# A new task order and new engine choices for the attention half of a fused attention and two-layer expert kernel

## The chip, the cores and the metric

The kernel runs on one core of one Trainium2 chip. The metric is the device time of one execution in microseconds (us). The kernel before took 1091.92, 1090.54 and 1091.52 us in three runs; their median is 1091.52 us.

## The reference

```python
def _attn_ref(q, k, v, tau):                     # 4 batches, 8 heads, 576 rows, head size 64
    scores = (1.0 / np.sqrt(64)) * np.matmul(q, k.transpose(0, 1, 3, 2))
    thresh = np.max(scores, axis=-1, keepdims=True) - tau
    scores = np.where(scores >= thresh, scores, -1e9)
    attn = np.exp(scores - np.max(scores, axis=-1, keepdims=True))
    attn = attn / (np.sum(attn, axis=-1, keepdims=True) + 1e-09)
    return np.matmul(attn, v)

def _moe_ref(x, w_gate, w_val, w_out):           # x: 2304 x 512, d_ff 1536
    gate = 1.0 / (1.0 + np.exp(-(x @ w_gate)))
    return (gate * (x @ w_val)) @ w_out

def _moe2_ref(x, w_in, w_out):                   # d_ff 2048
    h = x @ w_in
    return (h * np.cos(h)) @ w_out
```

The attention output is brought to 2304 x 512 and goes through the two layers in turn. Everything is float32, and the weights come as 64-bit floats.

## The kernel before

To keep float32 precision at the matmul's faster rate, an operand is split into a rounded high part and the rest, the low part, and a product is summed from high x high, high x low and low x high. Each split costs an activation (high part, ScalarE) and a subtraction (low part, VectorE or GpSimd).

The program has two halves. The first does attention for all 16 pairs of heads, and beside it the first products of layer one for the batches that are done. The second does the rest of layer one and all of layer two. Each half is a list of tasks of one engine each. `put_out` records the tasks engine by engine; where a string of letters is given for an engine (`ORDER`), the tasks are put out in just that order: a letter is a kind of task, and its n-th mention is the n-th task of that kind. The planner's own costs then have no say. An engine works off its queue in order, so a task that waits holds up all that stand behind it. The second half is ordered by another table (`LATER`).

In the first half a pair of heads has nine queries of 128 rows (144 in all). For one of them:

- S (TensorE, line 959): scores, 4 matmuls of 288 columns (6 for every ninth query) into one of two score banks `s`.
- M (VectorE, 965): the row's extreme `sm`. E (ScalarE, 970): exp from the bank into `p`. Y (any engine: 813, 815 or 817): the threshold. K (VectorE, 973): masks `p` by comparing the bank with the threshold. After K the bank is free for the next query but one.
- T, t (TensorE, 989 and 996): turns `p` by matmuls against the identity into one of two banks `t`. H, h (ScalarE, 899): the high part of the turned rows into `PT` or `LT`. The low part is made in one of three ways, by a letter in `LOWS` (for T) or `LOWS_L` (for t): V, a subtraction on VectorE (task L or l, line 910); G, a copy on ScalarE (task C, 914) and a subtraction on GpSimd (task G, 919); T, a matmul by minus the identity onto the bank (task N or n, 903) and a second activation (task O or o, 906).
- V (TensorE, 1056): the product with the values, four to a pair. Where `SHARED` has an S it takes 14 matmuls that write the result once (task a, 1017); else 9 that leave it in two halves, to be added by F (ScalarE, 1026) and A (VectorE, 1031).
- At the end of a pair the sums are inverted and spread, U scales `x` (1147), X and x split it into `xs_a` (1163 or 1165, and 1169). Then P (TensorE, 564 to 566) can run: products of layer one, three matmuls of 512 columns each, 144 of them; e (ScalarE, 1214) takes a sum out to `st` and it goes to memory.
- Before a pair, its q, k and v are split: s, Q, q for the queries (688 or 690, `qsplit` at 703 or 705, `ql` at 710), J and j for the keys (`khi`, `klo`), Z and z for the values (`vn`). Which engine does each is a letter for every pair in `WHERE`; that of Y is in `YS`.
- D (TensorE, 825): four matmuls on the identity that fill time, as many after a query's S as `FILL` says. b (ScalarE, 1183): loads the table for the sigmoid.

SyncE issues the transfers (loads, copies of split parts into place, `LZ`, sums) in an order of its own.

Of the kernel before, what the change touches and what calls it, by code (L numbers as in the profile page):

```python
# [52 lines left out]

ORDER = dict(
    PE=(
        "SDDDDSTSNDDDSTSNtTSnTStNSTTNSTtDDNSTStVNTtSSTBVtTSNSTTSVTtSSTVtNNSTStVnTTtNSTVBStSTVSTVTNSNtSTTNNSPtTPPStPST"
        "VTVStNSPTPPBSPPTPSStPTVTPStSVTTPSPtPTSPtPTPTVtSSTVPBTPtSPSTPPTPStSTVTVtSSTVNtVTTSPSPTPtSPPTBPSStPTPPSTtPSVTT"
        "SVtSPTPtSTVTVtSSPTBPPTtPSSTTVPtSPSTTVSPtSPPTPStTPTPVtTSSBVTPStPSPTPTSSPVtPSTPTPtVSPtTSPVTTSVtSPTPBPtSSTPPTTS"
        "StVPTTSStVVtTVnSTTSPtTPPBSPSPTPtSTVTtSVSTPTPPSTtPPSPTStVPTtPSSBTPVTtSPSTVTPSStPTPTSPSVPStPTPtSTPTVtPTPSSBPtT"
        "VPSSTTVtTVSTPSPTtPSPtVSTTVStPTSBPtPTPPSTPSVtTVSTTSPNNtPPSTSPPTPtSStPTPVTPSSBVTPtSSPTPTPStPTVSPTtSPVStPTPVTPT"  # L60
        "StSPTPBVtPTSSVTTVSPTtSPTPtSPPTPtSSPTTVSPtSTVPTBPStPTSPtTSVTVTSSVPtPTPtPPTPTPVtPBVBV"
    ),
    ACT=(
        "JQJQEYQsHEEOwHEOhECHo6EHhOEwHHHEOHhEOh6pHhEwEOHhCa6HEREhHwOEH6CHEEaahHwEYYHEHhOO6hHFhpEYoHHEhOwECFHRZhEYaHE6"
        "FwEHYaHOOhEHHH6OOwEhYhECehH6eHEEHFwFhOpEH6eREECweeHhEEHHe6hFEEYFHHHpwhheEHCEhe6CHHeFwhEHC6RFEHheHEEYHeheCEEF"
        "HHHFhhHYEOhFEFHpHECHheEERHeEehEHeYChHeEEHHCFEHhhFCHehHEpEFhHCFEHCREHheeHEEFChHEeHHEHFhhEeHCehEYHECHephFHCEER"
        "YFHhYsEEHeeCEHEFheHEHJhheHhFHEepEYFCHHEhYFEHYRehYHEEHeHChEEeCHHFhhEHFQFhHEopFHHCEhYHEReeEEHChHEeFHEhFHsHHQeY"
        "EHhhEeeHhpEEFChHesRHEEhCHeFEEYFHCHhEQEHHeYEHFEhhCHEhpHeHEFhHREEhCFHeYHHCEFhEHHFHEYhhHEYhEpeFCHHEFhHRCeEHCEeC"
        "heHEEhFHCFHHHEEOOhheCEHYEHeehEHEeFphCHXREEFHheEHEeHCheEZCHFEhheHHFEphHeECHHFhZeHEREeHhCYFEEFHHCFhECHHeHhEhEC"
        "heHpYEYEHCHehFHEEHRFhEHChHCeEECFHHHFFEhEhCHbhpeXHHXhFeFFX"  # L70
    ),
    DVE=(
        "jqMjqKqMMKKM4MK5MKYKMlMYYK4LL5MKYKllMMYlK4K5IlMMLKKM4l5KMMLKKlMML4K5KllMLMKLAYIlM4K5KMAMKLxlMA4KK5MYlMKxLM4K"
        "llK5MMYlLKKAM4lAI5KMLMYKK4M5MlKKLLMMAlKKALLLM4llM5IlKKLMA4l5MKAYKLMlMLKKLlMMKKALLAMllMKlAYKMLYAKIMLMlYKKLMMK"
        "lLKMMYlKKMALLllKAMMlLKKAMIlAMYKKlLMMLYKKMlAMKLYKAMLLlYlKMMlKYLKIlMMAKKAMLMlKKMMYKLAlMYLKKllLLMlAMLKKIMALMlAK"
        "KLMlMLKKLMlMYKKMMAllLLAKALKMLAMYlIKLKMMKYKMlYLKMLAYlMAKLLLMKllLKMMlLYKKIlAMMYLKKMjYlMAKKLMMlYKAKMLMKLLYAKllM"
        "YlMLLKIKlLAMMYYKKlMMALqKAlKMLLLAKMllMKLlMKAILKAlMMYYKKMlMYKYAKlAMLMKKMlYMlKKLMlMLKKIlAMMYKYKLMMAlKLMYlYKKMzA"
        "lKlMLLMAlYYILKKLlAMMYLYKKMMAlKYAKLMAlYKMLYLMllKKlMMKKLMMAlLIKKLMYlKAlMYMKYKALLAMMllAKKlILxlLAAUxAUxx"
    ),
    POOL=(  # L80
        "JJQYJYjYqZYzG7csQq7YJjYY7GYZ7YYzcGsQJ7qjUYsGXz7YQcUX7YqYJG7Y7jYYsYcQGZYqz7YJGY7GY7GjYUXZxYYsczQUXxGqJZYzYGjs"
        "cQGYJGYYqYGGYGjYsUcXYGQxZzJqGUXGxYjZYGQGqczYYZjsUXxYGzYcGGYYZUXxqzGYJjcGqYYGYJGcZzYqUGZzJjGYsGQGYZcUzXXxYxYJ"
        "GjGGGcYUYGsJjQGqYUYXxxGYGcsYQJqGzjGGGUcZGYGzUYGYGGGcYYGURRX"
    ),
    SP=(
        "10001W2uuuyWyuyy0ddssssW1uduuuW2ssssdyyrrW0y1RyssssRW2uu0uussssWrr1ddRRWyyy2yssssuuWgguu0Wssdssyydgg1WgyygDs"
        "sssrrWyggu2RRuugdrssrssuyd0RRyssssyggDu1u2d0gusygsrugss1dryyygsssysgRg2uuRu0dssssdg1ygurrgsgyyssRRsDuugg0ddu"
        "s2sssr1urygyyyDgg0ssssu2uRRyugyugDysssrrysgdg2ssssRRdu1gug0ssdrssdgguu2yDDgsyyrysssg10uuddRgssRssuugygyyy12s"
        "usssdguDrdryug0Ryussssr2rggD1RyssssdyRguu2uyRssss1yyudy0gsgDgssrrgRRs1gdys0gsdyrgrssguuuuDssyyDssgg2dgRRssss"
        "gg2uugrrdyyyuyusssRgsgRDssDssssssgrrRRgggDD"  # L90
    ),
)
# [1901 lines left out]
```

## Time and profile before

| | value |
|---|---|
| median of three runs | 1091.52 us |
| the profiled execution's own time | 1094.26 us |
| its span, first to last instruction | 1092.5 us |
| TensorE / VectorE / ScalarE / GpSimd busy | 98% / 83% / 70% / 50% |
| first product of layer one (line 564) begins | 70.84 us |
| first matmul of the second half (line 1441) begins | 384.95 us |

The span is that of one profiled execution; 1.8 us of the execution's time lie around it. The busy shares are means over both halves. A matmul's duration in the rows runs from its start to its modelled end, and matmuls overlap; what one costs the engine is the distance from its start to the start of the next.

### The profile page before, as it was taken

The numbers are of one execution on the slowest core, as the hardware profiler recorded it, in microseconds if no ns is written. First come the engines' busy times: TensorE is split into PE (matmuls) and PEld (weight loads), VectorE is DVE, ScalarE is ACT, GpSimd is POOL, SyncE is SP. The second block draws the span as 40 slices with busy tenths as digits, with TensorE's granted clock in tenths as the row PEclk, the third lists the DMA queues.
The fourth block names the chain that finished last, engine by engine and source line by source line (L and its number), as shares of the span: only waits on it lengthen the run. The fifth ranks groups of instructions, "written<-read, shape, count | busy, mean of one in ns | idle before, by whom it ended". The sixth has DMA issues, their size and how long they took to land.

```text
span 1092.5 us, 17726 instructions
## 1 busy us (share of the span) xinstructions
PE 1071.8 (98%) x5784; PEld 912.5 (84%) x5784; DVE 909.9 (83%) x1647; ACT 764.4 (70%) x1488; POOL 543.7 (50%) x521
## 2 busy tenths in 40 slices
...
GB/s 194 235 225 250 213 225 225 205 232 216 198 207 203 90 231 280 329 331 315 299 228 244 163 191 138 291 203 210 173 154 154 157 175 169 193 193 262 277 203 87
DMA packets 94494, 234.06 MB, mean 214 GB/s; under 512 B 13258, under 2 KB 21570, under 8 KB 84674
## 3 DMA queue, kind: packets, MB, share of 16 engines
...
q8 instruction: 46, 0.75, 0.3%
...
## 4 chain that ended last, share of the span: by engine, by line
PE 51%; DVE 2%; DMA 1%; ACT 1%; issue 0%; ACTq 0%
PE h L1441 5%; PE h L1442 5%; PE h L1443 5%; PE h L1630 4%; PE h L1631 4%; PE h L1632 4%; PE o L1750 4%; PE o L1751 4%; PE o L1752 4%; PE o L565 3%; PE o L566 3%; PE o L564 3%; DMA early<-gd 1%; PE o L1840 1%; PE o L1842 1%; PE o L1841 1%
## 5 line engine op out<-in xcount | busy, mean ns | idle before, releaser
L1676 POOL TENSOR_TENSOR g<-raws,g 128x512 fp32r<-128x512 f32 x68 | 94.7, 1402 | 139.7 <-ACT g L1675 117.6
L965 DVE TENSOR_REDUCE sm<-s 128x1 f32<-128x576 f32 x144 | 106.5, 751 | 8.9 <-PE s L959 7.2
L973 DVE SCALAR_TENSOR_TENSOR p<-s,sm,p 128x576 f32<-128x576 f32 x128 | 102.7, 812 | 9.3 <-ACT p L970 3.9
L1441 PE MATMUL h<-x,w 128*128 128x256 f32 (+1 forms) x304 | 101.4, 333 | 0.4 <-DVE raws L1718 0.4
L1442 PE MATMUL h<-x,w 128*128 128x256 f32 (+1 forms) x304 | 101.3, 333 | 0.0
L1443 PE MATMUL h<-x,w 128*128 128x256 f32 (+1 forms) x304 | 101.3, 333 | 0.0
L970 ACT ACTIVATE p<-s,sm 128x576 f32<-128x576 f32 x128 | 93.8, 742 | 9.8 <-DVE sm L965 9.0
L899 ACT ACTIVATE PT<-t 128x512 fp32r<-128x512 f32 (+1 forms) x160 | 86.1, 557 | 15.1 <-PE t L989 10.3
L959 PE MATMUL s<-kk,qh 128*128 128x288 f32 x320 | 92.4, 320 | 2.9 <-DVE p L973 2.5
L1056 PE MATMUL v<-PT,vn 128*128 128x256 f32 (+3 forms) x532 | 84.7, 302 | 0.2 <-ACT st L1214 0.2
L919 POOL TENSOR_TENSOR PT<-praw,PT 128x512 fp32r<-128x512 f32 x51 | 66.7, 1307 | 35.4 <-ACT praw L914 16.9
L1760 DVE TENSOR_TENSOR y<-o,y 128x512 f32<-128x512 f32 x120 | 78.6, 681 | 6.1 <-PE o L1752 5.9
L959 PE MATMUL s<-khi,ql 128*128 128x288 f32 x288 | 81.0, 295 | 0.6 <-DVE ql L670 0.6
L989 PE MATMUL t<-ident,p 128*128 128x128 f32 x512 | 77.0, 276 | 3.2 <-DVE PT L910 1.7
L1750 PE MATMUL o<-g,w 128*128 128x512 f32 x196 | 76.8, 392 | 0.5 <-ACT o L1766 0.5
L1751 PE MATMUL o<-g,w 128*128 128x512 f32 x196 | 76.4, 390 | 0.0
L1752 PE MATMUL o<-g,w 128*128 128x512 f32 x196 | 76.3, 389 | 0.0
L1630 PE MATMUL h<-form,w 128*128 128x512 f32 x192 | 75.0, 390 | 0.5 <-ACT side L1599 0.5
L1056 PEld LDWEIGHTS v<-PT,vn 128*128 128x128 f32 (+1 forms) x532 | 73.3, 186 | 2.2 <-DVE x L1031 0.5
L1631 PE MATMUL h<-form,w 128*128 128x512 f32 x192 | 74.7, 389 | 0.0
L1632 PE MATMUL h<-form,w 128*128 128x512 f32 x192 | 74.7, 389 | 0.0
L1675 ACT ACTIVATE g<-raws 128x512 fp32r<-128x512 f32 x106 | 64.3, 624 | 13.1 <-DVE raws L1718 8.3
...
## 6 DMA issues: line engine op xcount, KB each, us to landing
...
```

Source lines behind the costliest of these rows:

```text
L959: nc.tensor.matmul(s[:, half, 0:HALF], qq, keys[:, half * HALF:half * HALF + HALF], start=(i == 0), stop=(i == len(mms) - 1),)
L965: nc.vector.tensor_reduce(self.sm()[:, 0:1], self.s()[:, :, 0:HALF], axis=AX.XY, op=ALU.min)
L1056: nc.tensor.matmul(o, w, x, start=z == 0, stop=z == len(steps) - 1)
L1441: nc.tensor.matmul(o, w_hi, x(0, c), start=begin, stop=False, **late)
L1442: nc.tensor.matmul(o, w_hi, x(1, c), start=False, stop=False, **late)
L1443: nc.tensor.matmul(o, w_lo, x(0, c), start=False, stop=c == KC - 1, **late)
L1630: nc.tensor.matmul(ps(), of(0, c), hi, start=fresh and c == 0, stop=False, skip_group_check=True)
L1631: nc.tensor.matmul(ps(), of(0, c), lo, start=False, stop=False, skip_group_check=True)
L1632: nc.tensor.matmul(ps(), of(1, c), hi, start=False, stop=c == 1, skip_group_check=True)
L1750: nc.tensor.matmul(ps(), of(0, c), hi, start=begin, stop=False, skip_group_check=True)
L1751: nc.tensor.matmul(ps(), of(0, c), lo, start=False, stop=False, skip_group_check=True)
L1752: nc.tensor.matmul(ps(), of(1, c), hi, start=False, stop=True, skip_group_check=True)
```

## The change

The change replaces tables of letters and nothing else: the strings of `ORDER` for all five engines, `LOWS`, `LOWS_L`, `SHARED`, `WHERE`, `YS` and `FILL`. The arithmetic, the tiles, the planner and the second half's table are the same. A few lines show the kind:

```diff
 ORDER = dict(
     PE=(
-        "SDDDDSTSNDDDSTSNtTSnTStNSTTNSTtDDNSTStVNTtSSTBVtTSNSTTSVTtSSTVtNNSTStVnTTtNSTVBStSTVSTVTNSNtSTTNNSPtTPPStPST"
+        "SDDDDSTSNDDDSTtSNTSnDtTnSNSTTNSTDDDStTSNtVTSStTVBTtSNnSTTStVTSTSVtNSNStTVTTStNBTVSStTnVTSTVTtSnSTNtSPTPPSPTS"
...
 SHARED = (
-    "SSS. .S.S .... .... .... .... .... .... .... .... .... .... .... .... .... .... "
+    "SS.S S..S .... .... .... .... .... .... .... .... .... .... .... .... .... .... "
...
-    Q="APPPPPPPPPAAAPPP", q="DPPPPPPPPPPPPDPP", J="APPPPPPPPAPPPPPP", j="DPPPPPPPPPPDPPPP",
+    Q="APAPAAAAAPAAPPPP", q="DPPPPPPPPPPPPPPP", J="APPPPPPPPPPPPPPA", j="DDPPPPPPPPPPPPPP",
```

Counted over the first half, the tables change these numbers of tasks:

| engine | before and now |
|---|---|
| TensorE | N 18 to 11 (512 columns: 12 to 9; twice 256 columns: 6 to 2), n 3 to 6, D 9 to 11 |
| ScalarE | O 18 to 11, o 3 to 6, C 51 to 54, Q 6 to 11, s 4 to 5, Z 3 to 4, X 4 to 5, Y 29 to 27 |
| VectorE | low parts of 256 columns 26 to 30 and of 128 columns 61 to 58, U on full rows 0 to 2, x 6 to 7, q 4 to 3, Y 53 to 57 |
| GpSimd | G 51 to 54, Q 12 to 7, U 15 to 13, s 11 to 10, Z 13 to 12, X 12 to 11, x 10 to 9, q 14 to 15, Y 62 to 60 |

A bank's T with two halves has two pieces of each kind. The shared products stay five (three of 256 and two of 320 columns).

VectorE near the program's start, before the change; `klo` is the low part of a pair's keys, `wt` a piece of the layer's weights:

```order
L517 TENSOR_SCALAR wt<-wraw 128x512
L965 TENSOR_REDUCE sm<-s 128x1
L973 SCALAR_TENSOR_TENSOR p,sums<-s,sm,p 128x576
L520 SCALAR_TENSOR_TENSOR wt<-we,wt 128x512
L965 TENSOR_REDUCE sm<-s 128x1
```

The same place now:

```order
L965 TENSOR_REDUCE sm<-s 128x1
L973 SCALAR_TENSOR_TENSOR p,sums<-s,sm,p 128x576
L710 TENSOR_TENSOR klo<-raw_k,khi 128x640
L520 SCALAR_TENSOR_TENSOR wt<-we,wt 128x512
L965 TENSOR_REDUCE sm<-s 128x1
```

The second pair's `klo`, which GpSimd made before, now stands in VectorE's queue.

TensorE at the 86th to 88th query before, from the first instruction behind the 86th query's scores to the last of the 87th's (scores `s_3510`); behind them stand a T, a V, a T and a t, and then the 88th's scores, which take the 86th's bank:

```order
L564 MATMUL m_3477<-xs_a_98,w_554 128x512
L565 MATMUL m_3477<-xs_a_98,w_554 128x512
L566 MATMUL m_3477<-xs_a_98,w_554 128x512
L989 MATMUL t_3489<-ident_65,p_3366 128x128 x4
L996 MATMUL t_3508<-ident_65,p_3366 128x128
L959 MATMUL s_3510<-kk_2990,qh_1_100 128x288 x2
L959 MATMUL s_3510<-khi_2947,ql_1_102 128x288
```

The same place now, from the last instruction of the 86th's scores (`s_3511`) to the first of the 88th's (`s_3576`):

```order
L959 MATMUL s_3511<-khi_3020,ql_1_102 128x288
L959 MATMUL s_3523<-kk_3154,qh_1_100 128x288 x2
L959 MATMUL s_3523<-khi_3020,ql_1_102 128x288
L989 MATMUL t_3539<-ident_65,p_3479 128x128 x4
L989 MATMUL t_3546<-ident_65,p_3479 128x128 x4
L1056 MATMUL v_3556<-PT0_3270,vn_3033 128x320 x8
L1056 MATMUL v_3556<-LZ_3459,vn_3033 128x320
L959 MATMUL s_3576<-kk_3154,qh_1_100 128x288
```

Between a query's scores and the next in the same bank there stood two P tasks, two turns, a t, a V and one query's scores more; now two turns, a V and one query's scores.

ScalarE at the end of the first half, before:

```order
L1183 ACT_TABLE_LOAD
L1183 ACTIVATE one<-halfpi 128x1
L899 ACTIVATE LT<-t 128x128
L1069 ACTIVATE sums<-sums 128x9
L1214 ACTIVATE st<-m 128x512
L1163 ACTIVATE xs_a<-x_97 128x512
L899 ACTIVATE PT_5725<-t 128x4x128
```

And now:

```order
L899 ACTIVATE PT_5789<-t 128x4x128
L899 ACTIVATE LT<-t 128x128
L1163 ACTIVATE xs_a<-x_97 128x512
L1214 ACTIVATE st<-m 128x512
L1026 ACTIVATE half<-v 64x256
L1026 ACTIVATE half<-v 64x320 x2
L1183 ACT_TABLE_LOAD
L1183 ACTIVATE one<-halfpi 128x1
L1163 ACTIVATE xs_a<-x_97 128x512
```

The table load stood ahead of the last high parts; now only the last `xs_a` stands behind it in this half. TensorE ends the half with six P tasks behind the last query's scores, where it had eight.

## Rows read from the trace of the kernel before

**Rows 1.** The page: busy time, share of the span, instructions.

```profile
span 1092.5 us, 17726 instructions
...
PE 1071.8 (98%) x5784; PEld 912.5 (84%) x5784; DVE 909.9 (83%) x1647; ACT 764.4 (70%) x1488; POOL 543.7 (50%) x521
```

**Rows 2.** Stretches: length; busy PE, PEld, DVE, ACT, POOL; clock, DMA, GB/s.

```profile
8.00:71.00 63.00, 54.70 (x375) 46.56 (x374) 59.49 (x128) 56.29 (x122) 46.16 (x54) 1.00 0.82 223
...
71.00:380.00 309.00, 304.82 (x1978) 266.28 (x1977) 277.31 (x646) 264.58 (x578) 205.47 (x238) 1.00 0.75 208
```

**Rows 3.** Waits of TensorE, first 388 us: releaser, total, times, longest.

```profile
PE s L959 <- DVE p L973: 2.5, 6, 0.7
```

**Rows 4.** TensorE in order of time: start, duration, what.

```profile
8.44 1.91 PE L825 MATMUL warm<-ident 128*128 128x128 f32 x16
...
202.31 0.40 PE L566 MATMUL m<-xs_a,w 128*128 128x512 f32 x1
202.55 0.39 PE L564 MATMUL m<-xs_a,w 128*128 128x512 f32 x1
...
203.23 1.03 PE L989 MATMUL t<-ident,p 128*128 128x128 f32 x8
204.18 0.40 PE L959 MATMUL s<-kk,qh 128*128 128x288 f32 x1
```

**Rows 5.** VectorE by line and shape, first 388 us: busy, mean ns, idle before.

```profile
L965 DVE TENSOR_REDUCE sm<-s 128x1 f32<-128x576 f32 x144 | 106.5, 751 | 8.9 <-PE s L959 7.2
L973 DVE SCALAR_TENSOR_TENSOR p<-s,sm,p 128x576 f32<-128x576 f32 x128 | 102.7, 812 | 9.3 <-ACT p L970 3.9 <-POOL sm L815 2.5 <-ACT sm L813 0.3
L910 DVE TENSOR_TENSOR PT<-t,PT 128x512 fp32r<-128x512 f32 x65 | 44.5, 685 | 5.8 <-ACT PT L899 5.0
L910 DVE TENSOR_TENSOR LT<-t,LT 128x128 fp32r<-128x128 f32 x61 | 17.2, 281 | 2.7 <-ACT LT L899 2.3
...
L817 DVE TENSOR_SCALAR sm<-sm,taus 128x1 f32<-128x1 f32 x53 | 10.6, 205 | 0.4
...
L710 DVE TENSOR_TENSOR klo<-raw_k,khi 128x640 fp32r<-128x640 f32 x1 | 1.9, 1939 | 0.0
...
L710 DVE TENSOR_TENSOR vn<-raw_v,vn 128x640 fp32r<-128x640 f32 x1 | 0.8, 812 | 0.0
```

**Rows 6.** ScalarE by line and shape, same stretch and columns.

```profile
L970 ACT ACTIVATE p<-s,sm 128x576 f32<-128x576 f32 x128 | 93.8, 742 | 9.8 <-DVE sm L965 9.0
...
L703 ACT ACTIVATE qsplit<-raw_q 128x576 fp32r<-128x576 f32 x3 | 2.1, 686 | 0.0
```

**Rows 7.** In time: the first product of layer one and its releaser.

```profile
69.82 0.69 DVE L1169 TENSOR_TENSOR xs_a<-x,xs_a 128x512 fp32r<-128x512 f32 x1
...
70.84 0.40 PE L564 MATMUL m<-xs_a,w 128*128 128x512 f32 x1
```

**Rows 8.** In time: VectorE's `klo`, and what GpSimd ran beside it.

```profile
245.74 1.94 DVE L710 TENSOR_TENSOR klo<-raw_k,khi 128x640 fp32r<-128x640 f32 x1
...
245.71 1.29 POOL L919 TENSOR_TENSOR PT<-praw,PT 128x512 fp32r<-128x512 f32 x1 [2.26 <-ACT PT L899]
```

**Rows 9.** In time: the end of the first half.

```profile
370.89 0.28 PE L1056 MATMUL v<-LZ,vn 128*128 128x256 f32 x1
371.48 0.47 PE L564 MATMUL m<-xs_a,w 128*128 128x512 f32 x1 [0.31 <-DVE x L1031]
...
375.00 1.28 ACT L1183 ACT_TABLE_LOAD   x1
...
379.88 0.40 PE L566 MATMUL m<-xs_a,w 128*128 128x512 f32 x1
380.36 0.41 PE L1103 MATMUL t<-ident,bc 128*128 128x128 f32 x2
380.97 1.43 PE L1056 MATMUL v<-PT,vn 128*128 128x320 f32 x8 [0.19 <-ACT st L1214]
...
384.95 0.49 PE L1441 MATMUL h<-xs_a,w 128*128 128x512 f32 x1
```

More of the change, by code (lines that the diff above doesn't have):

```diff
@@ L55 @@
     PE=(
-        "SDDDDSTSNDDDSTSNtTSnTStNSTTNSTtDDNSTStVNTtSSTBVtTSNSTTSVTtSSTVtNNSTStVnTTtNSTVBStSTVSTVTNSNtSTTNNSPtTPPStPST"
[L57 to L60, printed above, removed]
@@ L61 @@
-        "StSPTPBVtPTSSVTTVSPTtSPTPtSPPTPtSSPTTVSPtSTVPTBPStPTSPtTSVTVTSSVPtPTPtPPTPTPVtPBVBV"
+        "SDDDDSTSNDDDSTtSNTSnDtTnSNSTTNSTDDDStTSNtVTSStTVBTtSNnSTTStVTSTSVtNSNStTVTTStNBTVSStTnVTSTVTtSnSTNtSPTPPSPTS"
+        "tVTVtSnSPTPBPSSTPPtTPSSTtPVPTSTPVtPSTtPSPTTPVPtTSSBPVTPtSSPTTPPStPSVTTVtSSTVtNVTTSPtSPPTPSBPStTPPSSPPTTPSStV"
+        "TTVPStPTStVTTVSPtSPTPBSPTtPSTTPSVTtVStPSTPPTPSSTPtVtTPSBSTPVtPTSSPTPTSStVPTPSTtVSPTPtSTPTPtVSTSPVTBPtSSPTPTS"
+        "tSVTPSPVtTSVTStVTTPStPTPBSPPtTPSSTTVStTVTPSPPStPPTPtSSPTVTPStSTPBVTPtSSPTPTSVtSPTTPSSVtPSTPSPtTPTVtSPTBPStPV"
@@ L62 @@
+        "TPSSTTVtTVTStPSPTPStPTVSTSVPtTPPSPSBTPtSVTTPStSTVPTSPtPSTtPPSTTPPStPVTSBPSPVTStPSPPTTSPVTtSPSPtTVSPTPtVSTTSP"
+        "tVPBTStSPTPVTSSTVPtTSTPPSPPtTPStPTVTSPtTSVPBTPStTPStPTVSVTSVtPTPSPTPPtPTPTPtVBVBV"
     ),
     ACT=(
-        "JQJQEYQsHEEOwHEOhECHo6EHhOEwHHHEOHhEOh6pHhEwEOHhCa6HEREhHwOEH6CHEEaahHwEYYHEHhOO6hHFhpEYoHHEhOwECFHRZhEYaHE6"
-        "FwEHYaHOOhEHHH6OOwEhYhECehH6eHEEHFwFhOpEH6eREECweeHhEEHHe6hFEEYFHHHpwhheEHCEhe6CHHeFwhEHC6RFEHheHEEYHeheCEEF"
-        "HHHFhhHYEOhFEFHpHECHheEERHeEehEHeYChHeEEHHCFEHhhFCHehHEpEFhHCFEHCREHheeHEEFChHEeHHEHFhhEeHCehEYHECHephFHCEER"
@@ L67 @@
[L67 to L70, printed above, removed]
+        "QJJQEYQsHEEwOHhEOEHCo6hEHwOoEHHHYOEQHE6hhHpEYhwEOHCa6hHEERHhwOoEHCHaEYhEF6HHwEYEHhhOpOahCHE6HHEhOEwRHaZhFH6E"
@@ new lines @@
+        "EYoFCHHwEahHo6EHOEHhhQwECH6eeHphEEHFhCowFEYERCHe6HEEhHeewCEEHFh6eHHEYQwHhhehHpCFEeHH6EFehCHwREE6HhesFEHEHehe"
+        "EYEFHCHHFQhhHEhOFEHpCFHhYEEeHReEEhCeHEEHHeQehEFHEHHFhheCHhEFHEHCpFhEeHsERECHhQeHHeEEFhCHFhhHHEEHCepeHEhEhZHF"
+        "eRHEEheHCEECFHHeEhEFYHCeHhhHFEHChEpHeEHFheHCEEYFRHhesEEHCHheXEQFHCEYEeFHHhhFHphCEFHHEheHYREEYeChHQeEHCHEFhCH"
+        "FHHEeEYhheEHehEYpHEHFehZHCEERHehFEEYHHYhEFECeHHEEHhhpCHFEYhHeHEFhRHshEEHFeHCHEFhECHZhhHHEFCHEhEpFeHEHCYFhHEC"
+        "eERHehEEHHehFEEFHHCHhhEeYhHepYEHCEeHehECFRHEEYFeHhEEeHHCYEeHFhCJEhehHHFEHYEheFHHCphEEFReChHEHEFHeEHCFhEHHHEe"
@@ L71 @@
+        "eEhhHpChEHCHFehHCEERCHFHChhEeCEHYFFCHEFEhHHHhCEhXepHHhXeFXFFbX"
     ),
     DVE=(
[L73 to L76, printed above, removed]
@@ L77 @@
-        "YlMLLKIKlLAMMYYKKlMMALqKAlKMLLLAKMllMKLlMKAILKAlMMYYKKMlMYKYAKlAMLMKKMlYMlKKLMlMLKKIlAMMYKYKLMMAlKLMYlYKKMzA"
-        "lKlMLLMAlYYILKKLlAMMYLYKKMMAlKYAKLMAlYKMLYLMllKKlMMKKLMMAlLIKKLMYlKAlMYMKYKALLAMMllAKKlILxlLAAUxAUxx"
+        "qjMjqKqMYMKK4MYMKj5MKYKM4MKLL5MKLKMllMKl4K5MMIlLKKM4Y5KMLMKlKAMMLKKll4MMl5YYKILMlKYK4L5MAMLKKMAL4Y5KMMKxLLYM"
+        "K4Y5lKlMMlLIKKAMM4AKK5MMYLKKlLM4M5KAlMLKKLLll4M5lAMKLLIKAlMM4Y5KKLlMMAYYKLKMlLMKKALLMAllYMlKAxKMALMlIKKLMMYK"
+        "KlMMYYKKLLMMlKALKLLlAlMMlYKALKMIAlKMLMYYKKlMYLLMKUAlKMAMYLLKKllMMIYLlKKlLAMYMLYKKlMMYKKAMLYMlKAKLllMLMKAlMYL"
@@ L79 @@
+        "KLKMAMlIYKKALMlMKKMlLKMAMKKALLllMAMlIxKLLAKlMLMKKlMMKLKlAMYALLKMMllKKLMMlYKLKLMlAIMYYKKLMAMlKKLMLlMKYKAMMYKL"
+        "LYKllMAMlKILLAlKLMYMlKKLAMMLYYKlAKMllLLKMAYMYKlKMAMILAlKKMYKMLMlKKLLMlAMYYKKAMLLllMKlLMIKKMYLlKMYAMKKAMYlLMK"
+        "LMKKlMAMKlLLlMAKLlKAMLMlIYKKMMYYALKKlMMALKAlKMLLLMKlYlMlKKLAIMMlYKUKAMlYlMKzKAAMMYYKKLLAMYllKlILxLlAxUAAUxx"
     ),
     POOL=(
-        "JJQYJYjYqZYzG7csQq7YJjYY7GYZ7YYzcGsQJ7qjUYsGXz7YQcUX7YqYJG7Y7jYYsYcQGZYqz7YJGY7GY7GjYUXZxYYsczQUXxGqJZYzYGjs"
-        "cQGYJGYYqYGGYGjYsUcXYGQxZzJqGUXGxYjZYGQGqczYYZjsUXxYGzYcGGYYZUXxqzGYJjcGqYYGYJGcZzYqUGZzJjGYsGQGYZcUzXXxYxYJ"
@@ L83 @@
-        "GjGGGcYUYGsJjQGqYUYXxxGYGcsYQJqGzjGGGUcZGYGzUYGYGGGcYYGURRX"
-    ),
-    SP=(
[L86 to L90, printed above, removed]
+        "JJQqYJYG7YcsZzYqJ7YZGYY7jsGQYqc7YzJjU7sGXzY7xGUYXc7JjqYYGZ7YGGsYz7YYc7GqYJGY7jY7UXZxzGYcGJUXYqjYZsYGzYJcjYGq"
@@ new lines @@
+        "YZGYzGGqYcJXYGxUYXGxjGYscGQzGYYqJZGjzGUYYYGqcYGxUYXsGYJjZGYYGqcGzJYjYUGsczQGqJUjYZQzYGGcqYGXXGxxJYjGGUYYscQq"
+        "GXJzYjUGXxxZzGGYcsQYYjqGGYZGzcUYYGYYGGGYGGZGcUGGRR"
+    ),
+    SP=(
+        "1000W21uuuuW0yy1ydydssssW2uuddWu0ussssyyWyrry1ssssuuRR0W2duussssrrWRR1yDWyydyssss2yWg0ug1WyurrssssugugWddyys"
+        "sssugg0Wyg2uRRssgyrygrssu1uddyssssRRgguu2gyDd0Dsysssggyrruyu1dDgR2ssssyRy1uug0guuddssgyssgryr02RRgsDsssgggsg"
+        "rrs1dssduuuyyRugyyssss2guuuRddg0ssgryrssuyRRgysssysuug0gd21guudssssyryr1gRygg0ssDyssgdyR21Dggyuususrssygyusd"
+        "Drus2RsRs0gyuuuyssgddss2rryyssss1dgRRgudguDssss01uurryyDyyDgggdRssugRuss0gg1y2uusrrsdssyyyggg2ssssggdduuuRgR"
+        "ssssyyy2grurygRssssgRggDssrssDDrssssRRgggDD"
```

14 lines of the change are left out of this document (7 added, 7 removed).

## The prediction

> **What bounds the kernel now.** I read the page's head first: over the whole span TensorE is busy 98% of the time, VectorE 83%, ScalarE 70% [rows 1]. That is a mean of two halves, so next the table by stretch. Only what runs before 384.95 us can change in itself, since the second half begins there and keeps its order [rows 9]. The first half has two parts. From 71 us on TensorE is busy 304.8 of 309 us, and VectorE and ScalarE have 31.7 and 44.4 us of idle time [rows 2]: TensorE is the bound. From 8 to 71 us TensorE is busy 54.7 of 63 us and VectorE 59.5 (94%) [rows 2]. There VectorE with the handoffs around it is the bound, and TensorE's 8.3 idle us are what a better order could win. The part ends when the products of layer one begin at 70.84 us, 0.3 us behind the last `xs_a` that they need [rows 7]; from then TensorE has work to fill its gaps.
>
> The waits of TensorE come third: the largest single kind is a score's wait for the mask that frees its bank, 2.5 us in all [rows 3]. A busy TensorE isn't one at its peak: a matmul of 512 columns has a duration of 0.40 us, but the next one starts 0.24 us behind it [rows 4]. I price its work by such distances.
>
> The sum is made for the profiled execution: 1094.26 us, with 1092.5 of span and 1.8 around it. It lies 2.7 us above the median of 1091.52, so its difference is taken over to the median.
>
> **The change, part by part.**
>
> *TensorE's own work.* Low parts made by a matmul with minus the identity fall from 12 to 9 of 512 columns and from 6 to 2 of 256, and rise from 3 to 6 of 128. At 0.24 us for 512 columns [rows 4], 0.12 for 256 (an estimate, half of it) and 0.12 for 128 (eight turns take 0.95 us from start to start [rows 4]) that is -0.72 - 0.48 + 0.36 = -0.84 us, in a half where TensorE is nearly always the bound. The shared products keep their number and widths: nothing. Two more fillers are eight matmuls, 0.12 us each (16 in 1.91 [rows 4]), 0.9 us; they stand behind scores of the first pair, where TensorE idles anyway, so nothing, and 0.9 if the work behind them is ready.
>
> *Work moved to VectorE and ScalarE.* VectorE gets four more low parts of 256 columns, two scalings, four thresholds and an `xs_a`, and gives up three small low parts and a `ql`; ScalarE gets five splits of queries at 0.69 us and three copies of 512 columns [rows 6] and loses the second activations of the lower matmul count. Each is some 3 to 4 us more in the half. From 71 us on the idle 31.7 and 44.4 us hide it: nothing. If that idle time is only handoff and can't be filled, the 3 us of VectorE come on top; I keep that as an upper bound.
>
> *The start, up to the first product.* Here VectorE's queue counts. Up to the last `xs_a` low part that the first product needs, it gains one `klo` (0.81 us as `vn` of the same size, or 1.94 as the only `klo` that VectorE made so far), two low parts of 512 columns (2 x 0.685) and a threshold (0.205), and loses three low parts of 128 (3 x 0.281) and one `xs_a` (0.69): between +0.9 and +2.0 us [rows 5, 7]. Against it stand VectorE's 3.5 idle us there (63 - 59.5 [rows 2]), of which a better order may win about half, -1.8. So the start is worth -1.8 to +2.0 us; I take +0.4, since VectorE at 94% has little to give and the added work is certain. Why `klo` took 1.94 us is seen beside it: GpSimd's subtraction had begun 0.03 us earlier and ran 1.29 us, and 1.94 is 1.26 of waiting and 0.68 of work [rows 8]. The Trainium skill's page "SBUF — State Buffer", in the section on its two separate sides, has this as a rule: a VectorE operation with two SBUF inputs and a GpSimd operation that reads SBUF share one port pair, and the later one stands still until the first is done. The trace agrees: 1.94 against 0.81 us. By that rule, two scalings and a `klo` on VectorE among GpSimd's work could each lose a GpSimd operation's 1.29 us, and the sum would be up to 3 x 1.29 = 3.9 us later if VectorE had no slack.
>
> *The score banks, later.* A bank is free again after the extreme, exp and mask of its query: at least 0.751 + 0.742 + 0.812 = 2.3 us and three handoffs [rows 5, 6]. I counted along TensorE's queue, with distances as above, how much work lies between a query's scores and the next scores in the same bank. Behind the first product, less than 3.0 us lies between in 2 places before and in 7 now; the 86th query is one at about the limit: two turns (0.95 us [rows 4]), a V (1.4 us, as the eight wide matmuls of 1.43 [rows 9]) and six score matmuls (0.14 each by width, an estimate). Five more places cost nothing if the mask is on time, and one VectorE instruction, 0.8 us, each if it is late: 0 to +4.0. The waits that stand in the trace after 71 us, 4.2 us of TensorE's idle time [rows 2], could as well shrink by a third, -1.4. I take +0.4, near the end where the masks are mostly on time: the trace has only six waits of this kind and the longest is 0.7 us [rows 3].
>
> *The end of the half.* TensorE's starts leave gaps: 370.89 to 371.48 for one matmul of 0.12, 379.88 to 380.36 for one of 0.24, 380.36 to 380.97 for two of 0.12 [rows 9], together 0.47 + 0.24 + 0.37 = 1.1 us. The table load of 1.28 us with its activation stands on ScalarE in the midst of this, ahead of the last high parts [rows 9]. Now it stands behind the last `half`, where ScalarE waits for VectorE; the `xs_a` part behind it is needed by the second half only behind its first 36 matmuls, some 8 us at 0.24 each. So between 0 and -1.5 us (the load and its activation in full). Two P tasks fewer behind the last scores (6 instead of 8, 1.4 us of cover) would bring idle time back if the last chain of extreme, exp, mask, turn and low part were later than the work that covers it; VectorE has few instructions left there. I take -0.8.
>
> Sum: -0.84 + 0.4 + 0.4 - 0.8 = -0.84 us. The profiled time would be 1093.4, the median 1091.52 - 0.84 = **1090.7 us**: no change that can be measured, since about 0.2% (2.2 us) is what a measurement of this kernel can tell from none.
>
> **The rivals.**
>
> *Faster: the start's waits go.* If the order fits the real durations better, half of TensorE's 8.3 idle us before 71 us may go: -4.2 in place of +0.4, with the other terms 1090.7 - 4.6 = 1086.1; with a quarter gone, 1088.2. For it: short distances between scores in one bank are fewer at the start (9 under 2.6 us, 11 before). Against it: VectorE's queue to the first product got longer, and it can't be more than full.
>
> *Slower: the score banks.* In the seven tight places, and at the start, the next scores wait for a mask that stands behind one more VectorE instruction: +4.0 in place of +0.4, and the start at its +2.0 instead of +0.4 because VectorE is full there: 1090.7 + 5.2 = 1095.9. It decides itself where the mask of the query two before ends later than the work between; TensorE's time is lost then, since it has no slack to take it back. For it: VectorE and ScalarE have more work in the half, 3 to 4 us each. Against it: the waits of this kind are short so far.
>
> *Slower because GpSimd holds VectorE.* VectorE's added `klo` and two scalings each stand still for a GpSimd instruction of 1.29 us, as the old `klo` did [rows 8], and TensorE with them: 1090.7 + 3.9 = 1094.6. (The skill's rule on the shared port pair, above, says that they can.) Against it: `vn` on VectorE shows no such wait (0.81 [rows 5]), and a scaling on VectorE is far from TensorE's next need.
>
> *The tables do little:* the letters change places among tasks that had slack, TensorE issues the same work, and the time is 1091.5. This has the same answer as my forecast.
>
> **How the numbers follow.** No measurable change, 1089.3 to 1093.7: 0.42 (my terms, or none of them). Faster: 0.36, most of it with a quarter to a half of the start's waits gone, 1086.1 to 1089.3. Slower: 0.22, of which 0.17 by the score banks and 0.05 by GpSimd's hold on VectorE. The terms' own ends add up to 1091.52 - 0.84 - 1.8 - 1.4 - 1.5 = 1086.0 and 1091.52 - 0.84 + 0.9 + 2.0 + 4.0 = 1097.6; not all ends come together, so the range that should hold the time 8 times in 10 is 1086.5 to 1095.0. The forecast's own range is 1089.3 to 1093.7.
>
> **What would show it.** The first product of layer one should begin at 70.8 + 0.4, within 2 us; earlier than 68.5 means the faster rival. The first matmul of the second half should begin near 384.1. From 71 us to there TensorE's idle time should stay near 4 us; with the score banks as the brake, the waits of line 959 for line 973 grow from 2.5 us to 5 or more. At the end no gap of TensorE should be left by the table load. VectorE's `klo` for the second pair should take 0.8 us, or more if GpSimd's instruction began first. I am wrong if the first half's length changes by more than 2.2 us either way, or if the second half's does at all.

## The result, and the profile after

The changed kernel is slower: 1099.96 us (median of six runs, 1099.19 to 1105.89) against 1091.13 us for the kernel before beside it. The ratio of the means is 1.0095, with a 95% interval of 1.0071 to 1.0120. In two of the six runs, the profiled one among them, TensorE's granted clock was a little lower (0.997 of full speed over the run), and they took some 5 us longer; the other four lie between 1099.2 and 1100.1, so the trace shows more than the 8.8 us between the medians.

The page's head, against [rows 1]:

```profile
span 1104.1 us, 17719 instructions
...
PE 1075.2 (97%) x5788; PEld 915.5 (83%) x5788; DVE 918.9 (83%) x1654; ACT 767.6 (70%) x1493; POOL 538.7 (49%) x512
```

The stretches of [rows 2], then finer ones (length; busy PE, PEld, DVE, ACT, POOL; clock, DMA, GB/s):

```profile
8.00:71.00 63.00, 54.89 (x367) 47.11 (x367) 59.30 (x123) 53.51 (x117) 40.97 (x47) 0.97 0.77 210
71.00:380.00 309.00, 296.90 (x1912) 259.53 (x1912) 275.30 (x635) 259.28 (x563) 197.34 (x227) 0.99 0.74 207
...
40.00:71.00 31.00, 26.28 (x174) 23.52 (x173) 28.81 (x61) 26.11 (x59) 21.82 (x24) 0.94 0.75 196
71.00:110.00 39.00, 33.11 (x193) 28.07 (x193) 34.61 (x71) 30.49 (x69) 24.60 (x30) 0.96 0.74 199
110.00:150.00 40.00, 36.93 (x238) 31.73 (x237) 35.23 (x82) 32.99 (x70) 26.52 (x29) 1.00 0.80 224
150.00:310.00 160.00, 157.35 (x1036) 138.80 (x1035) 145.41 (x341) 137.01 (x298) 103.76 (x122) 1.00 0.75 212
```

The same stretches of the kernel before:

```profile
40.00:71.00 31.00, 27.20 (x187) 23.65 (x185) 29.54 (x64) 28.75 (x66) 24.84 (x28) 1.00 0.86 227
71.00:110.00 39.00, 38.42 (x247) 33.17 (x246) 36.76 (x86) 36.46 (x80) 27.78 (x33) 1.00 0.85 245
110.00:150.00 40.00, 39.40 (x261) 34.37 (x260) 35.93 (x84) 32.84 (x72) 30.79 (x38) 1.00 0.79 216
150.00:310.00 160.00, 157.85 (x1025) 138.12 (x1024) 145.46 (x335) 135.74 (x298) 106.92 (x122) 1.00 0.78 215
```

TensorE issues 54 matmuls fewer between 71 and 110 us, and is alike from 150 us on. The second half begins 12.5 us later than in [rows 9] and takes 706.6 us in place of 707.5:

```profile
397.49 0.49 PE L1441 MATMUL h<-xs_a,w 128*128 128x512 f32 x1
```

So nearly all of the loss lies between 40 and 150 us. The waits of TensorE in the first 399 us name the releaser, against [rows 3]:

```profile
PE s L959 <- DVE p L973: 10.2, 11, 2.2
```

Five of these waits are over 1 us. Three of them (1.25 us at 29, 1.95 at 56 and at 81 us) come behind VectorE instructions that stand still; the longest, 2.2 us at 138 us, comes behind one that waits for its input from GpSimd. VectorE's lines by shape (busy, mean ns, idle before), in the kernel before:

```profile
L520 DVE SCALAR_TENSOR_TENSOR wt<-we,wt 128x512 uint32<-128x512 uint32 x12 | 9.4, 784 | 0.0
L517 DVE TENSOR_SCALAR wt<-wraw 128x512 uint32<-128x512 uint32 x12 | 5.3, 438 | 0.1
```

and in the changed one:

```profile
L520 DVE SCALAR_TENSOR_TENSOR wt<-we,wt 128x512 uint32<-128x512 uint32 x12 | 12.3, 1027 | 0.0
L517 DVE TENSOR_SCALAR wt<-wraw 128x512 uint32<-128x512 uint32 x12 | 8.4, 700 | 0.1
```

These are the two steps that bring a weight piece from 64 to 32 bits, 12 pieces in both kernels. Alone they take 0.69 and 0.42 us. In the changed kernel nine VectorE instructions (eight of these and a low part of `xs_a`) take 8.2 us more than that, all before 95 us; in the kernel before it is some 1.4 us, and 1.1 us for the `klo` of [rows 8]. Two places, in time (start, length; the last brackets: idle before, and what ended it):

```profile
50.14 1.58 POOL L710 TENSOR_TENSOR klo<-raw_k,khi 128x640 fp32r<-128x640 f32 x1
50.28 1.73 DVE L517 TENSOR_SCALAR wt<-wraw 128x512 uint32<-128x512 uint32 x1
...
53.26 1.40 POOL L1147 TENSOR_TENSOR x<-x,bc 128x576 f32<-128x576 f32 x1 [1.54 <-DMA bc<-rd]
53.58 1.63 DVE L520 SCALAR_TENSOR_TENSOR wt<-we,wt 128x512 uint32<-128x512 uint32 x1
...
55.44 0.82 DVE L973 SCALAR_TENSOR_TENSOR p<-s,sm,p 128x576 f32<-128x576 f32 x1
...
56.32 0.40 PE L959 MATMUL s<-kk,qh 128*128 128x288 f32 x1 [1.95 <-DVE p L973]
...
77.02 1.57 DVE L517 TENSOR_SCALAR wt<-wraw 128x512 uint32<-128x512 uint32 x1
...
78.69 1.74 DVE L520 SCALAR_TENSOR_TENSOR wt<-we,wt 128x512 uint32<-128x512 uint32 x1
...
81.35 0.40 PE L959 MATMUL s<-kk,qh 128*128 128x288 f32 x1 [1.95 <-DVE p L973]
```

At the first place a weight step twice begins 0.1 to 0.3 us behind a GpSimd subtraction or scaling and ends only 0.3 to 0.6 us behind that one's end. The mask behind them comes late, and TensorE waits 1.95 us for it. It is what [rows 8] showed of `klo`. How much is held differs from run to run: the run with the fourth `xs_a` moved (below) has the same order up to some 125 us, and its trace, of an execution of 1097.99 us, shows 5.2 us of hold before 95 us and

```profile
PE s L959 <- DVE p L973: 4.4, 8, 1.2
```

in place of 10.2; 2.2 us of the difference is the place at 138 us that this run moved. I call it the second trace. In the changed kernel a low part of `xs_a` is held as well, near the first product, against [rows 7]:

```profile
73.08 1.28 POOL L529 TENSOR_TENSOR w<-wt,w 128x512 fp32r<-128x512 f32 x1
73.41 1.50 DVE L1169 TENSOR_TENSOR xs_a<-x,xs_a 128x512 fp32r<-128x512 f32 x1
...
73.47 0.30 PE L996 MATMUL t<-ident,pl 128*128 128x128 f32 x1 [0.89 <-ACT PT L906]
...
74.24 0.40 PE L564 MATMUL m<-xs_a,w 128*128 128x512 f32 x1
...
75.72 0.63 PE L989 MATMUL t<-ident,p 128*128 128x128 f32 x4 [0.61 <-DVE sm L817]
```

The first product does not wait for it: it begins at 74.24 us, and the held subtraction ends at 74.91. TensorE's wait ahead of the product, 0.89 us, is put down to ScalarE; behind the subtraction a turn waits 0.61 us for VectorE. In the kernel before, too, TensorE ran scores up to its first product at 70.84 us and did not stand idle ahead of it:

```profile
70.71 0.29 PE L959 MATMUL s<-khi,ql 128*128 128x288 f32 x1
```

The `klo` that moved to VectorE, which I had thought at risk, was not held; no GpSimd instruction ran beside it:

```profile
18.76 0.82 DVE L710 TENSOR_TENSOR klo<-raw_k,khi 128x640 fp32r<-128x640 f32 x1
```

Behind TensorE's two waits of 1.95 us its granted clock fell in the profiled run, from 58.8 to 62.2 us and from 82.7 to 86.1 us, to 0.50 of full speed: the lower of its two levels, 1.2 GHz (windows as above):

```profile
50.00:55.00 5.00, 4.15 (x32) 3.71 (x32) 4.92 (x7) 3.10 (x8) 3.04 (x3) 1.00 0.79 197
55.00:60.00 5.00, 3.19 (x16) 2.52 (x17) 4.83 (x15) 4.65 (x10) 3.85 (x4) 0.88 0.83 220
60.00:65.00 5.00, 4.89 (x29) 4.45 (x27) 3.65 (x7) 3.37 (x8) 2.27 (x3) 0.78 0.40 98
...
58.80:62.15 3.35, 3.35 (x18) 3.35 (x17) 2.67 (x9) 2.40 (x6) 1.79 (x3) 0.50 0.56 130
82.70:86.05 3.35, 3.35 (x18) 3.35 (x17) 3.10 (x9) 2.36 (x5) 2.98 (x5) 0.50 0.93 279
```

A score matmul then starts 0.24 us behind the last in place of 0.13 us, so each fall costs up to 1.7 us (an estimate: half of such a stretch). The second trace has no such fall.

To compare kernels I call TensorE's *lost time* the distance from a matmul's start to the next one's, less the usual one for its shape, which is the median in the kernel before (0.227 us for 512 columns, 0.133 for a score, 0.109 for a turn). By stretch, up to the second half:

```
                          8-40  40-71  71-110  110-150  150-end   all
before                     9.0    7.3     2.4      3.1     15.4  37.2
changed                    8.5    9.3    10.1      5.6     16.2  49.7
second trace               8.5    8.4     4.9      4.4     15.5  41.8
```

The usual distances themselves come to 339.8 and 339.7 us before and now: TensorE's own work didn't change.

### The profile page after: what moved, and what is told of

It is laid out like the page before. It is cut to its first block, busy times and chain, and to the rows that moved or that the text cites. A ratio compares the mean times of both kernels' runs of the same rounds, so it can differ in the third digit from the quotient of the medians.

```text
span 1104.1 us, 17719 instructions
## 1 busy us (share of the span) xinstructions
PE 1075.2 (97%) x5788; PEld 915.5 (83%) x5788; DVE 918.9 (83%) x1654; ACT 767.6 (70%) x1493; POOL 538.7 (49%) x512
## 4 chain that ended last, share of the span: by engine, by line
PE 83%; DVE 7%; ACT 4%; DMA 3%; issue 2%; POOL 1%; SPq 1%; DVEq 0%; ACTq 0%; POOLq 0%
PE h L1441 7%; PE h L1442 7%; PE h L1443 7%; PE s L959 6%; PE v L1056 5%; PE o L564 5%; PE o L565 5%; PE o L566 5%; PE h L1630 4%; PE h L1632 4%; PE h L1631 4%; PE o L1750 4%; PE o L1752 4%; PE o L1751 4%; PE t L989 4%
## 5 line engine op out<-in xcount | busy, mean ns | idle before, releaser
L959 PE MATMUL s<-kk,qh 128*128 128x288 f32 x320 | 93.0, 321 | 11.6 <-DVE p L973 10.2
L919 POOL TENSOR_TENSOR PT<-praw,PT 128x512 fp32r<-128x512 f32 x54 | 69.6, 1288 | 39.6 <-ACT praw L914 23.0
L1056 PE MATMUL v<-PT,vn 128*128 128x256 f32 (+2 forms) x532 | 86.2, 306 | 0.1
L959 PEld LDWEIGHTS s<-kk,qh 128*128 128x128 f32 x320 | 58.7, 190 | 24.9 <-DVE p L973 12.9
L1056 PEld LDWEIGHTS v<-PT,vn 128*128 128x128 f32 (+1 forms) x532 | 75.8, 192 | 2.3 <-DVE x L1031 0.6
```

The costliest lines, as they stand in the source:

```text
L959: nc.tensor.matmul(s[:, half, 0:HALF], qq, keys[:, half * HALF:half * HALF + HALF], start=(i == 0), stop=(i == len(mms) - 1),)
L1056: nc.tensor.matmul(o, w, x, start=z == 0, stop=z == len(steps) - 1)
```

## The experiments

Ratios are to the kernel before, with a 95% interval; 0.001 is 1.09 us. My theory: GpSimd holds VectorE, and the new order puts the weight steps in its way. The rivals: the order sets scores of one bank too close, or VectorE and ScalarE have too much work.

**The weight steps in another form, in both orders.** In the first half the two steps become (second output: a sum)

```diff
+ nc.vector.tensor_scalar(f32(self.t)[:, 0:256], self.e[:, 0:256], 1.0, 0.0, op0=ALU.mult, op1=ALU.add, accum_out=junk[:, 0:1])
...
+ nc.vector.tensor_scalar(f32(self.t), self.e, 1.0, 0.0, op0=ALU.mult, op1=ALU.add, accum_out=junk[:, 1:2])
```

> The kernel before, with the two VectorE instructions of each weight piece of the first half (lines 517 and 520) written in another form: one SBUF input and a sum as second output, over 256 and 512 columns. It leaves out the lowest 3 bits of the weights of the first half. Theory (GpSimd holds the old form): in the kernel before only two pieces are held, 1.1 us in all, so the time is within 1.5 us of the kernel before; the new instructions take about 0.35 to 0.45 and 0.6 to 0.7 us, and none takes over 0.2 us more than its like. Rival (the old form costs nothing by itself, only the order counts): the same time too; this run is the base of the next one. If the new form is held as well, one or two of its instructions still take over 1.1 us, and the pair of runs tells nothing of the theory.

> The changed kernel with the same edit of lines 517 and 520, which leaves out the lowest 3 bits of the weights of the first half. Theory (the changed order puts these instructions just behind GpSimd's, eight of them stand still for 7.3 us of VectorE, and TensorE waits for it): without the hold the loss of 8.8 us falls to 1 to 3 us against the kernel before (the low part of xs_a, another 0.8 us, stays held), and the product of layer one begins 5 to 6 us earlier than in the changed kernel. Rival one (the order brings scores of one bank too close together, and VectorE and ScalarE have more work): the loss stays at 7 to 9 us. Rival two (both half): 4 to 5 us.

(These, and two further down, say that the lowest 3 bits are left out. It is more: the shift by three places is missing too, so the weights of the first half have other values.)

Measured: 1.0074 (1.0061 to 1.0086) in the old order, 1.0115 (1.0098 to 1.0132) in the new. The first missed: it should have cost nothing. But its first half ended at 382.40 us, and its second half took 715.4 us, 8 more, as in every kernel with the small tile `junk`. The run with that tile alone, below, gives 1.0080, so the form itself costs nothing and the new order then costs 0.0035 to 0.0041, some 4 us, in place of 0.0095. That is what I had expected of the hold and the rest of the order together (4 to 5 us), not of the hold alone (1 to 3). No weight step is held any more; the same one as above, in the new order and the other form:

```profile
48.73 1.59 POOL L717 TENSOR_TENSOR klo<-raw_k,khi 128x640 fp32r<-128x640 f32 x1
48.90 0.42 DVE L519 TENSOR_SCALAR_CACHE_REDUCE wt<-we 128x256 f32<-128x256 f32 x1
```

The first product begins at 69.67 us. TensorE's wait for the mask falls from 10.2 us, or 4.4 in the second trace, to 3.5 (line 973 is 980 here; 1.8 in the old order and this form), and the lost time from 49.7, or 41.8, to 39.8 us. So two traces don't tell the hold's price. The ratios do: by them it is 0.0054 to 0.0060, some 6 us and over half of the loss, though only to within 3.5 us. Scores too close are not the cause of this part. Of the rest they could be up to 1.7 us (3.5 less 1.8); that was not tested.

**The small tile alone.**

```diff
+    junk = const.tile([P, 2], F32, tag="junk", name="junk")
+    nc.gpsimd.memset(junk, 0.0)
```

> The kernel before with nothing but an 8-byte tile that is cleared once and not used, at the place where the kernels with the other form have it. Theory (the 8 bytes shift the later tiles, and the second half's matmuls run slower by it): 7 to 9 us slower, 1.0065 to 1.008, all in the second half, and the kernel with the other form in the order of before (1.0074) then costs nothing by its form. Rival (the other values of the weights, or the form, did it): within 1 us of the kernel before.

Measured: 1.0080 (1.0066 to 1.0094), the first half as before (382.65 us), the second 714.8 us. Its matmuls run slower one by one, in the kernel before

```profile
L1630 PE MATMUL h<-form,w 128*128 128x512 f32 x192 | 75.0, 390 | 0.5 <-ACT side L1599 0.5
```

and with the tile

```profile
L1632 PE MATMUL h<-form,w 128*128 128x512 f32 x192 | 76.1, 397 | 0.3 <-ACT side L1601 0.3
```

and they start 0.234 us apart in place of 0.227. Over all 2747 matmuls of 512 columns in that half it is 0.231 in place of 0.227 and 7.9 us in all.

**Only the seven steps that are held longest, in the other form.** First with the 8-byte tile, then with one of 128 bytes.

> The changed kernel, in its own order, with only the seven weight instructions that GpSimd holds for over 0.6 us (first step of the pieces 5, 8 and 9, second step of 2, 5, 8 and 9; 7.0 us together) in the form that is not held; the second half is untouched. It leaves out the lowest 3 bits of the weights of these pieces. Theory one (a us of VectorE costs about 0.55 us, as the two kernels with the other form and the pieces moved say): 3.5 to 5 us faster than the changed kernel, 1.0049 to 1.0063 of the kernel before. Theory two (a us costs 1.1, as the added instructions in the kernel before say): the whole loss goes, 1.0005 to 1.003. Rival (the hold costs nothing of its own): 1.008 to 1.0095.

> The same as the run with the seven instructions in the form that is not held, but the small tile that takes their sums has 128 bytes in each partition in place of 8. The weights of these seven steps get other values in it: the shift by three places and the low bits are left out, as in all kernels with this form (not only the lowest 3 bits, as was said there). In the four kernels with the 8-byte tile the second half took 715.2 to 715.4 us in place of 706 to 708.6. If the 8 bytes did that by shifting all later tiles, the second half is back at 706 to 708 here. Then the price of the hold can be read from the whole time: by the first-half lengths of the earlier runs 1.0060 to 1.0080 of the kernel before (1.3 to 3.5 us faster than the changed kernel); the hold as the whole loss would be 1.0005 to 1.003, no price 1.0095.

Measured: 1.0143 (1.0125 to 1.0161) and 1.0131 (1.0115 to 1.0146). Both have the long second half; 128 bytes don't cure it, so my idea of the 8 bytes fell, and why later tiles are slower when shifted stays open. Less the tile's 1.0080, the loss is 0.0063 and 0.0051: 3.5 and 4.8 us are won, each within about 3.5 us, since the changed kernel's own time is known to 2.7 us only. That is theory one's 3.5 to 5. The hold is not the whole loss, and by the second run it is not nothing; the first alone can't tell.

**The other way round: the old order, with VectorE made longer at those steps.**

> The kernel before with the weight instructions in the other form (its base is the run of that, 1.0074 of the kernel before), and to seven of them VectorE instructions of the same form are added behind, 8.4 us in all: 1.36 us at the first step of pieces 5, 8 and 9, and 1.09 us at the second step of pieces 2, 5, 8 and 9. These are the steps that GpSimd holds in the changed kernel, for 7.0 us; the order is that of the kernel before. It leaves out the lowest 3 bits of the weights of the first half. Theory (lost time of VectorE there costs about 0.55 us for each us, as the pieces moved showed): 4 to 6.5 us slower than its base, all of it before 110 us. Rival (VectorE has the slack in the old order, and only the new order is sensitive): under 2 us.

Measured: 1.0160 (1.0146 to 1.0174), 9.4 us above its base for the 8.4 us added: more than I expected, and the rival is out. Lost time rose from 6.7 to 9.0 us between 40 and 71 us and from 2.7 to 7.8 between 71 and 110, and elsewhere by about 1 us at most. Part of it is the clock, which fell to 0.50 from 52.1 to 55.5 us in the profiled run (up to 1.7 us) and not in the base. Between 71 and 110 us it stayed at 1.00: there 5.0 of the 8.4 us were added, and 5.1 us more were lost. VectorE has no slack there in the old order either.

**The pieces moved in VectorE's order.** A few letters of the string change places, so that a weight step (4, 5) begins ahead of a GpSimd subtraction; for instance

```diff
-KAMMLKKll4MMl5YYK
+KAMMLKK4llMMl5YYK
```

> The changed kernel with seven of the eight held weight instructions, and the held low part of xs_a, moved by one to three places in VectorE's order, away from the start of a GpSimd subtraction; nothing else. Theory: VectorE wins back 4 to 7 of 8 us there, and the time falls by 3 to 6 us against the changed kernel (a loss of 3 to 6 us against the kernel before stays; some other instruction may now be held). Rival (tight score banks, more work): the moves change less than 1 us, and the loss stays near 9 us.

> The pieces moved as in the run with seven pieces moved, but the second instruction of the eighth piece stands nearly at its old place: in that run ScalarE stood 3.5 us for it and TensorE lost 2.8 us at 76 us. Theory (the hold is about half of the loss, as the two kernels with the other form show by their first halves): 3 to 5 us faster than the changed kernel, a loss of 4 to 6 us stays. Rival (the order as such is the loss): within 1.5 us of the changed kernel.

Measured: 1.0070 (1.0057 to 1.0084) and 1.0060 (1.0047 to 1.0073). The first won 2.7 us, less than its theory, and it set one step too late: ScalarE stood for it, and TensorE behind ScalarE:

```profile
77.10 0.69 DVE L520 SCALAR_TENSOR_TENSOR wt<-we,wt 128x512 uint32<-128x512 uint32 x1
77.83 0.63 ACT L525 ACTIVATE w<-wt 128x512 fp32r<-128x512 f32 x1 [3.51 <-DVE wt L520]
78.36 1.06 ACT L1214 ACTIVATE st<-m 128x512 f32<-128x512 f32 x2
78.99 0.87 PE L1056 MATMUL v<-PT,vn 128*128 128x256 f32 x3 [2.61 <-ACT st L1214]
```

In the second, 1.7 us of hold are left of 8.2, and 3.8 us (about 3 either way) are won by an order alone: as expected, and by another way than the other form.

**Single places in the rest of the loss.** Five kernels move more tasks, alone or on top of the pieces (the letters of VectorE's, ScalarE's, GpSimd's and again VectorE's string):

```diff
-KAxKMAL
+KAKMxAL      fourth pair's low part of xs_a: in the first and second
-YQwHhhe
+YQHhhwe      eleventh piece's high part: in all but the first
-GUYXc7
+GUYcX7       two clearings of pl ahead of a high part: in the third and fifth
-K4L5MAMLKK
+K4L5MALMKK   a low part of PT ahead of an extreme: in the third
```

> The changed kernel with one VectorE task moved two places later: the low part of xs_a of the fourth pair (line 1169, at 136.78 us of the changed kernel) goes behind the mask and the extreme that follow it. Theory (it stands at the head of VectorE's queue 2.3 us ahead of its input, which GpSimd makes late, and the mask behind it frees the bank of the next scores): TensorE's wait of 2.2 us at 138.5 us goes, the time falls by 1.3 to 2.4 us. Rival (the mask or the low part is late for another reason, or the time is lost again at the next product): within 0.5 us of the changed kernel.

> The pieces moved as in the run before, the fourth low part of xs_a moved as in the first run of this call, and on ScalarE the high part of the eleventh weight piece (line 513, at 105.75 us) behind the three small high parts that stood behind it. Theory (three separate waits on queues, which add): 3 to 5 us by the pieces, 1.3 to 2.4 by xs_a, 0.5 to 1.0 by the weight piece: 5 to 8 us faster than the changed kernel, 1 to 4 us slower than the kernel before. Rival (TensorE waits elsewhere instead, since VectorE is full up to the first product): no more than 4 us are won.

> The changed kernel with the pieces moved as in the second run of that kind (1.0060 of the kernel before), and three more tasks moved by one to three places: ScalarE's high part of the eleventh weight piece (line 513) behind three small high parts; GpSimd's two clearings of pl (line 983) ahead of the high part of xs_a (line 1165) near 70 us; VectorE's low part of PT (line 910) ahead of an extreme near 61 us. Theory (what is left of the loss are single tasks that stand ahead of one for which TensorE waits): each wait of 0.6 to 1.1 us goes, 1.5 to 3 us faster than that run, 1.0032 to 1.0046. Rival (VectorE is full in this stretch, so that a wait that goes comes back at another place): within 1 us of that run.

> The changed kernel with the pieces moved as in the second run of that kind (1.0060 of the kernel before) and one more task moved: ScalarE's high part of the eleventh weight piece (line 513), which waited 1.3 us for its load with small high parts behind it, goes behind three of these. Theory (this wait is one of those that make up the rest of the loss, and TensorE's 0.8 us near 100 us are its price): 0.5 to 1.2 us faster than that run, 1.0049 to 1.0056. Rival (TensorE waits at that place for the transfer of ql as well, or later): the same as that run within 0.4 us.

> The changed kernel with the pieces moved and the load's high part moved (1.0058 of the kernel before), and GpSimd's two clearings of pl (line 983) ahead of the high part of xs_a (line 1165) near 69 us, with VectorE's mask ahead of the low part of xs_a as in the changed kernel, so that no mask waits for GpSimd. TensorE lost 1.3 us there to the clearing and 0.6 to the mask. Theory (single places make up the rest of the loss): 1.0 to 1.9 us faster, 1.0041 to 1.0049. Rival (the wait comes back at another place, as in the run with six places): 1.0055 to 1.009.

Measured: 1.0098 (1.0082 to 1.0115), 1.0079 (1.0067 to 1.0091), 1.0086 (1.0072 to 1.0100), 1.0058 (1.0040 to 1.0076) and 1.0060 (1.0048 to 1.0073). None reaches its theory. The fourth comes nearest, 0.2 us better than its base, which can't be told from no gain. The first shows why: the moved `xs_a` now starts behind a GpSimd `klo`, and the product waits for it.

```profile
129.65 1.58 POOL L710 TENSOR_TENSOR klo<-raw_k,khi 128x640 fp32r<-128x640 f32 x1
129.73 2.04 DVE L1169 TENSOR_TENSOR xs_a<-x,xs_a 128x512 fp32r<-128x512 f32 x1
...
131.83 0.51 PE L565 MATMUL m<-xs_a,w 128*128 128x512 f32 x1 [1.50 <-DVE xs_a L1169]
```

In the second, third and fifth run too an `xs_a` is held anew, for 1.3, 1.1 and 1.1 us; behind it the granted clock fell to 0.50 in the second (at 130.6 us) and the third (at 73.7 us). So a wait that goes comes back elsewhere, mostly as a hold; the 4 to 7 us that are left I could not put down to single places.

**The kernel before, mended.** The table load late, and then two weight steps out of GpSimd's way as well.

```diff
-EhCHbhpeXHHXhFeFFX
+EhCHhpeXHHXhFeFFbX
...
-YlK4K5IlMM
+YlK4KIl5MM
...
-ML4K5Kll
+ML4KK5ll
```

> The kernel before with one letter moved in ScalarE's order: the load of the sigmoid's table (line 1183) goes from the midst of the last splits to behind the last sum, ahead of the last high part of xs_a, as in the changed kernel. My term for the end of the half in its narrow sense: the table load of 1.28 us no longer delays the last products, -0.3 to -1.1 us. Rival (TensorE has other work while the table loads): no change, within 0.3 us. Other rival: the last high part of xs_a comes later and the second half waits for it, +0.5 to +1.3 us.

> The kernel before with the table load late, as tried, and two weight instructions of VectorE (at 33.56 and 48.42 us) moved one or two places later, out of the way of GpSimd instructions that held them for 0.65 and 0.48 us. Theory (a held VectorE costs TensorE about as much in the stretch where VectorE is full): 0.8 us by the table as before and 0.5 to 1.1 us by the pieces, 1.3 to 1.9 us faster than the kernel before. Rival (the two delays have slack): as the run with the table alone, 0.5 to 1.2 us.

Measured: 0.9992 (0.9984 to 1.0001) and 1.0003 (0.9994 to 1.0011). The first fits my 0.8 us and doesn't show it. In the second the hold of the weight steps is gone from the trace, and the time is not better, against the 1.3 to 1.9 us expected: 1.1 us of hold at 33 and 48 us is within what can't be measured. No version beats the kernel before.

## Why the prediction was wrong

I forecast 1090.7 us, no measurable change, and 1086.5 to 1095.0 as the range; the time is 1100.0. Point by point:

- *TensorE's own work*, -0.84: the usual distances came to 339.8 and 339.7 us. The smaller low parts are eaten up by eight more fillers, which I had put at 0.9 us and then at nothing. It is right that they stand where TensorE idles: its lost time from 8 to 40 us is 0.4 us less.
- *Moved work at nothing* is a step that failed. I took VectorE's 31.7 idle us behind 71 us for cover. Of the time added to VectorE in the old order 5.0 us lay between 71 and 110 us, and TensorE lost 5.1 us more there: that idle time is handoffs, at least up to 110 us. I had kept 3 us as an upper bound for this case. What the moved work costs by itself was not measured.
- *The start*, +0.4 (-1.8 to +2.0), is the step where the forecast broke. I counted what VectorE's queue gains and loses, each at its usual duration. The weight steps are neither gained nor lost, only placed elsewhere, so they did not enter the sum, here or behind the first product; 7.3 of the 8.2 us of hold are theirs. The first product came at 74.24 us in place of 71.2. In the second trace it came at 72.24, within the term's range, and most of the loss came behind it. Nor do [rows 7] show that the last `xs_a` released the product, as I read them: TensorE did not stand idle ahead of it, and now the product begins before that part is done.
- *The score banks*: the wait of line 959 for line 973 grew from 2.5 to 10.2 us (4.4 in the second trace), the sign that I had named for them. But the sign does not tell the cause. With the weight steps free it is 3.5 us in the new order.
- *The end of the half*, -0.8: the late table alone gave 0.9 us, with an interval that also holds no change, and the changed kernel's lost time from 310 us on did not fall (5.7 us; 4.9 before).
- *GpSimd holds VectorE* was the right mechanism with the wrong victims, at a chance of 0.05 and 3.9 us. I named the added `klo` (0.82 us, not held) and two scalings (0.75 us each, not held), because they were new on VectorE; that 3.9 us is near what the hold cost is luck. The Trainium skill's page "SBUF — State Buffer", section "SBUF: two separate sides", gives the lock to VectorE operations in a two-port mode as well as to those with two SBUF inputs. The trace agrees that two inputs are not needed: line 517, with one SBUF input, is held for up to 1.3 us. Whether it runs in such a mode no run shows; alone it takes 0.42 us for 512 columns, the time in which the form with the sum does 256, and that form is never held (at most 0.42 us for 256 columns and 0.69 for 512). I should have listed every VectorE instruction that can be held, with the GpSimd instruction that stands beside it in the new order.

Sum: of about 9 to 10 us, 3.5 to 6.5 are the hold, by three ways of taking it off, each known to some 3 to 3.5 us either way. The rest, 4 to 7 us, stays open. Its lost time lies for the most part between 40 and 150 us (in the new order with the form that isn't held, 16.5 us there against 12.2 in the old order); that the added work of VectorE and ScalarE makes it is only argued. The granted clock is little of it: the four runs of the changed kernel at 0.999 or more over the run lose 8 to 9 us too.
